# Second heads written to partitions 0 to 63, and a planner that counts the pause where the first partition changes

## The chip, the cores and the metric

The kernel runs on one core of a Trainium2 chip. The time is the device time of one execution in microseconds. Below, PE is TensorE's matmuls and PEld its weight loads, DVE is VectorE, ACT is ScalarE, POOL is GpSimd, and SP is SyncE, which here only issues DMAs.

## The reference

Attention with a decaying bias over 8 batches, 8 heads, 576 positions and 64 numbers a head, then a channel mix of the 512 joined numbers of each position with a hidden layer of 1024:

```python
scores = scale * np.matmul(q, k.transpose(0, 1, 3, 2))
cum = np.cumsum(np.maximum(s, 0.0), axis=-1)
bias = -(cum[:, :, :, None] - cum[:, :, None, :])
scores = np.where(causal, -1000000000.0, scores + np.minimum(bias, 0.0))
attn = np.exp(scores - np.max(scores, axis=-1, keepdims=True))
attn = attn / (np.sum(attn, axis=-1, keepdims=True) + 1e-09)
x = np.matmul(attn, v)          # heads joined: B, S, H * D
...
xk = mu_k * x + (1.0 - mu_k) * x_prev
xr = mu_r * x + (1.0 - mu_r) * x_prev
k = np.maximum(xk @ w_k, 0.0)
out = 1.0 / (1.0 + np.exp(-(xr @ w_r))) * (k * k @ w_v)
```

x_prev is x moved by one position.

## The kernel before

**Visits.** Attention goes over visits: one batch and one pair of heads. The first batch is done in two parts for each pair (eight visits in plain float32), the other seven batches in one visit for each pair, 28 in all, where each float32 operand is split into a rounded part and a rest (ph and pl for the weights of attention, the four column blocks of V for the values). A visit takes its two heads j = 0 and 1 one after the other. For each: PE multiplies queries and keys into a bank `s` (L743 plain, L754 split); DVE adds the mask, takes the row's extreme and frees the bank (L771, tile nm); ACT takes the exponential (L789); POOL divides by the sum (L803, L825); PE transposes the weights into a bank `t` (L847, L861); ACT and DVE split the transposed weights into ph and pl (L887 and L891 for whole blocks; L912, L916, L935, L943 and L955 for half blocks, of which one half lies on partitions 64 to 127 of the bank); PE multiplies them with the values into a bank `po` or the rest of a `t` bank (L995 plain, L1011 split); and ACT (L1041; L1034 plain) and DVE (L1045) add the two halves of that bank into xT.

**xT.** It is a tile of 128 partitions: head 0 of the pair on partitions 0 to 63, head 1 on 64 to 127. In the split visits ACT copies one half of the bank, the rows of the rest of V, to the head's partitions and DVE adds the other half. For head 0 ACT reads from partition 64 and writes at 0 and DVE stays at 0; for head 1 ACT reads from 0 and writes at 64, and DVE reads and writes at 64. The plain product of L995 multiplies the values of both heads and copies the rows of the one it wants. When both heads are done, one DMA (L1347) writes xT to x_d in DRAM.

**Mixing.** The 18 chunks of 256 positions read x_d back into the one tile x (L1240). For each pair of 128 channels ACT scales x by mu into the bank `xp` (L1087) and DVE adds the neighbour's share (L1096); a bank takes two such ACT steps and two DVE steps (more where a chunk lies across two batches), then ACT rounds the bank into xh (L1115) and DVE takes the rest xl (L1119). There is one `xp` bank. PE multiplies into the two `m` banks (L1148 hidden layer, L1190 gate, L1215 output); ACT and DVE square the hidden layer in four steps, r (L1160), m (L1170), kh (L1175) and kl (L1177), after which the bank is free; DVE joins gate and output (L1226), and a DMA writes the result (L1232). DVE, ACT and PE wait for each other through semaphores, also where two of them touch different parts of one bank.

**The planner.** No instruction is issued where the code names it. Each becomes a task with an engine, a length and what it reads and writes, and `Plan.run` simulates all engines with a table of costs, forward and backward in turn for eight passes, and issues all tasks in the order of the shortest pass. In each step the engine that is free first takes its most urgent ready task. SELF is the time from the end of a task to a dependent one on the same engine, AFTER and BEFORE the parts of it across engines. The order thus found is the order of every engine, the DMAs' SP included. A part of a buffer is named by a pair, as `(xm, (y, o))`; two tasks depend on each other where one writes a part that the other names.

## Time and profile before

| what | value |
|---|---|
| median of 3 runs | 890.72 us (886.85 to 893.18) |
| the profiled execution | 892.16 us |
| its span, first to last instruction | 890.4 us |
| mean granted clock of TensorE | 0.992 of full speed |
| busy: PE, PEld | 854.3 us (96%), 741.1 us (83%) |
| busy: DVE, ACT, POOL | 668.8 us (75%), 677.5 us (76%), 423.3 us (48%) |

Busy time is the union of an engine's instructions. Matmuls are pipelined, so a busy PE may still be slower than it could be. In a timeline, a line gives the start from the span's beginning, the length, and in square brackets the idle time before it with what ended it; the end of an instruction is its start plus its length, and where the next one starts before that, the two overlap. A wait names the engine and line that waited, the one that released it, the total in us, how often, and the longest.

### The profile page before, as it was taken

Reading aid. Unit: us, or ns where it says so; the run is one execution under the profiler, and the core shown is the slowest. Engines: PE = TensorE matmul, PEld = TensorE weight load, DVE = VectorE, ACT = ScalarE, POOL = GpSimd, SP = SyncE. Lnnn points to the kernel's source line nnn. Section 1 sums busy time; section 2 is a strip of 40 time slices with the busy share of each in tenths; the row PEclk is TensorE's granted clock in tenths of the full one; section 3 lists DMA queues with packets and bytes.
Section 4 is the critical chain, followed back from the end, with each engine's and each line's share of the span. In section 5 each row is a group of like instructions: output and inputs, shape, how many; then the busy total and the mean of one; then the engine's idle time right before and its main releaser. Section 6 shows DMA issues by size and latency. Waiting matters only on the chain.

```text
span 890.4 us, 16963 instructions
## 1 busy us (share of the span) xinstructions
PE 854.3 (96%) x5353; PEld 741.1 (83%) x5353; DVE 668.8 (75%) x2190; ACT 677.5 (76%) x1810; POOL 423.3 (48%) x654
## 2 busy tenths in 40 slices
PE   8899999999999999999999999989999999998998
PEld 6678788779798888979897989888888879987886
DVE  6989898789777887778877786868787768445431
ACT  5988999989878887888878787878787868346331
POOL 7655877865546455545455545443544532000000
PEclk8989999999999999999999999999999999999999
DMA  7887355453544525333334443242435110111100
GB/s 195 272 237 219 94 162 142 108 155 102 128 130 108 143 77 154 88 109 100 113 93 110 116 124 109 76 132 61 135 82 144 43 62 14 42 33 35 48 26 24
DMA packets 52762, 96.70 MB, mean 109 GB/s; under 512 B 7502, under 2 KB 20820, under 8 KB 52672
## 3 DMA queue, kind: packets, MB, share of 16 engines
q1 hardware_dynamic: 52672, 95.62, 38.5%
q8 instruction: 42, 0.69, 0.3%
q14 instruction: 48, 0.39, 0.2%
HBM read 67.85 MB, written 19.48 MB: 98 GB/s over the span
## 4 chain that ended last, share of the span: by engine, by line
PE 54%; DVE 18%; ACT 18%; issue 5%; DMA 2%; POOL 2%; SPq 1%; ACTq 0%; DVEq 0%; POOLq 0%
PE m L1148 17%; PE m L1215 11%; PE m L1190 7%; PE s L754 5%; PE po L1011 5%; ACT W L789 4%; DVE W L771 4%; PE t L847 4%; DVE xp L1096 4%; ACT xp L1087 3%; DVE pl L891 3%; ACT ph L887 3%; DMA x<-x_d 2%; DVE xT L1045 2%; PE po L995 1%
## 5 line engine op out<-in xcount | busy, mean ns | idle before, releaser
L1148 PE MATMUL m<-xh,w_k 128*128 128x256 f32 x1152 | 231.1, 286 | 2.5 <-DVE kl L1177 2.4
L789 ACT ACTIVATE W<-W,nm 128x448 f32<-128x448 f32 (+4 forms) x320 | 179.1, 561 | 27.8 <-DVE nm L771 24.4
L1215 PE MATMUL m<-w_v,kh 128*128 128x512 f32 x576 | 198.9, 403 | 0.4 <-DVE r L556 0.4
L1148 PEld LDWEIGHTS m<-xh,w_k 128*128 128x128 f32 x1152 | 185.8, 188 | 5.2 <-DVE kl L1177 2.7
L803 POOL TENSOR_SCALAR W<-W,rinv 128x192 f32<-128x192 f32 (+4 forms) x320 | 164.4, 532 | 32.7 <-DVE rinv L830 30.2
L1148 PE MATMUL m<-xl,w_k 128*128 128x256 f32 x576 | 163.2, 283 | 0.2 <-DVE xl L1119 0.2
L771 DVE CUSTOM_DVE_ANT_0 W<-s,causal 64x64 f32<-64x64 f32 (+4 forms) x320 | 128.3, 409 | 24.2 <-PE s L754 15.4
L1215 PEld LDWEIGHTS m<-w_v,kh 128*128 128x128 f32 x576 | 106.6, 188 | 18.0 <-DVE r L556 0.8
L891 DVE TENSOR_TENSOR pl<-t,ph 128x512 fp32r<-128x512 f32 x224 | 104.3, 485 | 19.7 <-ACT ph L887 18.1
L1215 PE MATMUL m<-w_v,kl 128*128 128x512 f32 x288 | 115.0, 399 | 0.0
L1096 DVE SCALAR_TENSOR_TENSOR xp<-x,mu,xp 128x256 f32<-128x256 f32 (+3 forms) x192 | 80.7, 420 | 44.6 <-ACT xp L1087 41.7
L847 PE MATMUL t<-ident,W 128*128 128x128 f32 x640 | 111.7, 276 | 2.1 <-POOL W L803 0.8
L754 PE MATMUL s<-KH,G 128*64 128x64 f32 x336 | 101.5, 310 | 11.3 <-DVE nm L771 11.2
L1087 ACT ACTIVATE xp<-x,mu 128x256 f32<-128x256 f32 (+3 forms) x192 | 81.5, 424 | 37.8 <-DVE xl L1119 13.4
L1148 PEld LDWEIGHTS m<-xl,w_k 128*128 128x128 f32 x576 | 108.5, 188 | 1.6 <-DVE xl L1119 0.6
L722 POOL TENSOR_TENSOR G<-raw,G 64x1152 fp32r<-64x1152 f32 x28 | 75.0, 2678 | 58.6 <-issue 42.3
L1190 PE MATMUL m<-w_r,xh 128*128 128x512 f32 x288 | 101.9, 405 | 0.1
L754 PE MATMUL s<-KL,G 128*64 128x64 f32 x336 | 97.9, 294 | 0.0
L887 ACT CAST ph<-t 128x512 fp32r<-128x512 f32 x224 | 89.1, 426 | 11.0 <-PE t L847 5.6
L847 PEld LDWEIGHTS t<-ident,W 128*128 128x128 f32 x640 | 80.1, 142 | 16.0 <-issue 2.9
L1011 PE MATMUL po<-ph,V 128*128 128x448 f32 x280 | 85.1, 319 | 4.5 <-ACT ph L887 4.2
L825 POOL TENSOR_SCALAR rinv<-sums 128x5 f32<-128x5 f32 (+2 forms) x72 | 17.3, 240 | 141.7 <-ACT W L789 138.8
(112 smaller groups left out, 1742.7 us busy)
## 6 DMA issues: line engine op xcount, KB each, us to landing
raw<-in_q SPq DMA_DIRECT2D x56, 288.0 KB
raw<-in_k SPq DMA_DIRECT2D x56, 288.0 KB
out<-g SPq DMA_DIRECT2D x36, 256.0 KB
vn<-in_v SPq DMA_DIRECT2D x28, 320.0 KB
x_d<-xT SPq DMA_DIRECT2D x28, 288.5 KB
G<-G SPq DMA_DIRECT2D x28, 288.0 KB
x<-x_d SPq DMA_DIRECT2D x12, 514.0 KB
w_k<-in_moe_w_k SPq DMA_DIRECT2D x8, 512.0 KB
```

The costliest lines, as they stand in the source:

```text
L754: lambda x=x, g=g, K=K: nc.tensor.matmul(ps.get()[:m, :w], g.get()[:, h % 2, q0 : q0 + m], K.get()[:, h % 2, k0 : k0 + w], start=x == 0, s ...
L771: lambda a=a, e=e, at=at, i=i: nc.vector.tensor_tensor_reduce(out=W.ap[:m, at : at + e - a], in0=ps.get()[:m, a - k0 : e - k0], in1=causal ...
L789: lambda: nc.scalar.activation(W.ap[:m, :n], W.ap[:m, :n], AF.Exp, bias=nm.get()[:m, 3 * t + mi : 3 * t + mi + 1], scale=-1.0, accum_out=s ...
L803: lambda: nc.gpsimd.tensor_scalar(out=to, in0=W.ap[:m, :n], scalar1=rinv.get()[:m, t : t + 1], scalar2=1.0, op0=ALU.mult, op1=ALU.mult,),
L847: lambda: nc.tensor.transpose(ps.get()[0:m, place : place + P], pt[t].ap[:, lead(t) + k0 : lead(t) + k0 + m], ident.ap),
L887: act(lambda: nc.scalar.copy(strips(ph), src()), [ps], [(ph, k) for k in ks], n * m)
L891: lambda: nc.vector.tensor_tensor(out=strips(pl), in0=src(), in1=f32(strips(ph)), op=ALU.subtract),
L1011: lambda: nc.tensor.matmul(po.get()[: P if both else 64, at + q0 - base : at + q0 - base + m], V.get()[:, kb, 2 * j : 2 * j + (2 if both e ...
L1096: lambda n=n, o=o, i=i, to=to: nc.vector.scalar_tensor_tensor(out=to(), in0=x.get()[:, c, o + i : o + i + n], scalar=mu1.ap[:, which, c : ...
L1148: lambda u=u, f=f, c=c, n=n, w=w, x=x: nc.tensor.matmul(ps.get()[:, u * CT : (u + 1) * CT], weight["k", c, f // 4].get()[:, w, f % 4 * P : ...
L1190: lambda c=c, n=n, x=x, w=w: nc.tensor.matmul(ps.get(), x.get()[:, c, ts], weight["r", c, 0].get()[:, w], start=c == 0 and n == 0, stop=c ...
L1215: lambda f=f, n=n, x=x, w=w: nc.tensor.matmul(ps.get(), x.get()[:, f, ts], weight["v", f, 0].get()[:, w], start=f == 0 and n == 0, stop=f ...
```

## The change

xT becomes a tile of 64 partitions with a second dimension for the head, so that both heads of a pair lie on partitions 0 to 63. In the split visits ACT reads from partition 64 and DVE adds from partition 0 for either head. The plain product takes one head's 64 columns of V. The DMA to x_d reads 64 partitions with two rows each.

The planner gets a short text for every ACT and most DVE tasks that says which memories it reads and writes and from which partition ("P64>S": from partition 64 of PSUM to partition 0 of SBUF). It keeps, for ACT and DVE, the first partition of the last read and write in each memory. A task for which one of them differs counts as held and is simulated 122 ns (ACT) or 108 ns (DVE) later; and of the up to four most urgent ready tasks the engine takes the one with the least due time, where a held one counts 200 ns later. SELF of DVE goes from 127 to 185 ns. In the mixing, the ACT steps of one bank now depend on each other through the part "a", the DVE steps through "d".

```diff
@@ -56,18 +57,20 @@
-    SELF = {"PE": 0.0, "ACT": 150.0, "DVE": 127.0, "POOL": 62.0, "SP": 0.0}
+    SELF = {"PE": 0.0, "ACT": 150.0, "DVE": 185.0, "POOL": 62.0, "SP": 0.0}
...
+    HELD, LOOK, AVOID = {"ACT": 122.0, "DVE": 108.0}, 4, 200.0
...
@@ -95,6 +98,27 @@
+
+    def side(self, i, ports):
+
+        if ports is None:
+            return
+        ins, out = (
+            [(x[0], int(x[1:] or 0)) for x in re.findall("[PS][0-9]*", part)] for part in ports.split(">")
+        )
+        self.ports[i] = ins, out
+
+    def held(self, i, state):
+
+        ins, out = self.ports.get(i, ((), ()))
+        return any(state["R" + m] != p for m, p in ins) or any(state["W" + m] != p for m, p in out)
+
+    def moved(self, i, state):
+        ins, out = self.ports.get(i, ((), ()))
+        for m, p in reversed(ins):
+            state["R" + m] = p
+        for m, p in out:
+            state["W" + m] = p
 
     def add(self, engine, ns, emit, reads=(), writes=(), land=0.0):
         i = len(self.tasks)
...
@@ -139,6 +163,7 @@
+        states = {e: dict.fromkeys(("RP", "RS", "WP", "WS"), 0) for e in self.HELD}
...
@@ -191,6 +216,19 @@
                     if x is not best:
                         heapq.heappush(ready[e], x)
                 i = best[1]
+            if e in self.HELD:
+                if ready[e]:
+                    some = [(due[i], i)]
+                    while ready[e] and len(some) < self.LOOK:
+                        some.append(heapq.heappop(ready[e]))
+                    best = min(some, key=lambda x: x[0] + self.AVOID * self.held(x[1], states[e]))
+                    for x in some:
+                        if x is not best:
+                            heapq.heappush(ready[e], x)
+                    i = best[1]
+                if self.held(i, states[e]):
+                    s += self.HELD[e]
+                self.moved(i, states[e])
             _, ns, _, _, _, land = self.tasks[i]
             if e == "PE":
 
...
@@ -339,11 +377,15 @@
-    def act(emit, reads, writes, n, extra=51, table=0):
-        return plan.add("ACT", n * 0.8333 + extra, emit, reads, writes, land=table)
-
-    def dve(emit, reads, writes, n, rate=0.96):
-        return plan.add("DVE", n / rate + 68, emit, reads, writes)
+    def act(emit, reads, writes, n, extra=51, table=0, ports=None):
+        i = plan.add("ACT", n * 0.8333 + extra, emit, reads, writes, land=table)
+        plan.side(i, ports)
+        return i
+
+    def dve(emit, reads, writes, n, rate=0.96, ports=None):
+        i = plan.add("DVE", n / rate + 68, emit, reads, writes)
+        plan.side(i, ports)
...
@@ -958,7 +1001,7 @@
                             in1=f32(ph.get()[0:64, c]),
                             op=ALU.subtract,
                         ),
-                        [ps, (ph, ("h", k1))], [(ph, "l")], 64,
+                        [ps, (ph, ("h", k1))], [(ph, "l")], 64, ports=f"P{64 * r}S>S64",
                     )
 
         def turned(*what):
...
@@ -986,21 +1029,19 @@
         else:
             turned((0, 2))
             turned([(3, 4)], (2,), (3,))
-        lo, ot = 64 * j, 64 * (1 - j)
-
         def values(po, base, at, kb, q0, m, x, first, last):
             parts = [("h", kb), "l" if kb == NQ - 1 else kb]
             if plain:
                 i = pe(
                     lambda: nc.tensor.matmul(
-                        po.get()[:, at + q0 - base : at + q0 - base + m],
-                        V.get()[:, kb],
+                        po.get()[0:64, at + q0 - base : at + q0 - base + m],
+                        V.get()[:, kb, j],
                         x.get()[:, col(kb, q0) : col(kb, q0) + m],
                         start=first,
                         stop=last,
                     ),
                     [V] + [(x, i) for i in parts[: 2 if kb < NQ - 1 else 1]],
-                    [po], m, P, 4 / 2.4,
+                    [po], m, 64, 4 / 2.4,
                 )
                 if plan.busy_from is None:
                     plan.busy_from = i
...
@@ -1031,24 +1072,22 @@
             n = q1 - q0
             if plain:
                 act(
-                    lambda: nc.scalar.copy(
-                        xT.get()[lo : lo + 64, 1 + q0 : 1 + q1], po.get()[lo : lo + 64, at : at + n]
-                    ),
-                    [po], [(xT, (j, q0))], n,
+                    lambda: nc.scalar.copy(xT.get()[:, j, 1 + q0 : 1 + q1], po.get()[0:64, at : at + n]),
+                    [po], [(xT, (j, q0))], n, ports="P>S",
                 )
                 return
             act(
-                lambda: nc.scalar.copy(xT.get()[lo : lo + 64, 1 + q0 : 1 + q1], po.get()[ot : ot + 64, at : at + n]),
-                [po], [(xT, (j, q0))], n,
+                lambda: nc.scalar.copy(xT.get()[:, j, 1 + q0 : 1 + q1], po.get()[64:P, at : at + n]),
+                [po], [(xT, (j, q0))], n, ports="P64>S",
             )
             dve(
                 lambda: nc.vector.tensor_tensor(
-                    out=xT.get()[lo : lo + 64, 1 + q0 : 1 + q1],
-                    in0=po.get()[lo : lo + 64, at : at + n],
-                    in1=xT.get()[lo : lo + 64, 1 + q0 : 1 + q1],
+                    out=xT.get()[:, j, 1 + q0 : 1 + q1],
+                    in0=po.get()[0:64, at : at + n],
+                    in1=xT.get()[:, j, 1 + q0 : 1 + q1],
                     op=ALU.add,
                 ),
-                [po], [(xT, (j, q0))], n,
+                [po], [(xT, (j, q0))], n, ports="PS>S",
             )
 
         for q0, q1 in sums_of(tiles):
...
@@ -1090,7 +1129,7 @@
                         AF.Copy,
                         scale=mu.ap[:, which, c : c + 1],
                     ),
-                    [(x, i), (mu, which)], [(xm, (y, o))], n, 160,
+                    [(x, i), (mu, which)], [(xm, (y, o)), (xm, "a")], n, 160, ports="S>P",
                 )
                 dve(
                     lambda n=n, o=o, i=i, to=to: nc.vector.scalar_tensor_tensor(
@@ -1101,7 +1140,7 @@
                         op0=ALU.mult,
                         op1=ALU.add,
                     ),
-                    [(x, i), mu1], [(xm, (y, o))], n,
+                    [(x, i), mu1], [(xm, (y, o)), (xm, "d")], n, ports="SP>P",
                 )
 
         def splits(c, xm, hi, lo):
...
@@ -1344,7 +1383,9 @@
 
             c = slice(1 + q0 if q0 else 0, 1 + q1)
             dma(
-                lambda: nc.sync.dma_start(x_d[b].ap[:, hp, c], xT.get()[:, c]),
+                lambda: nc.sync.dma_start(
+                    x_d[b].ap[:, hp, c].rearrange("(h d) t -> d h t", h=2), xT.get()[:, :, c]
+                ),
                 [(xT, 2)] + [(xT, (i, x)) for i in range(2) for x, _ in sums_of(tiles)],
                 [(x_d[b], (hp, y)) for y in range(2) if tiles is ALL or y == (q0 > 0)],
                 819,
@@ -1359,8 +1400,8 @@
         if 0 < n < len(visits) - 1:
             load(n + 1)
         plan.due = due
-        xT = sbuf([P, S + 1], "xT", 2)
-        pool(lambda xT=xT: nc.gpsimd.memset(xT.get()[:, 0:1], 0.0), [], [(xT, 2)], 1, 36)
+        xT = sbuf([64, 2, S + 1], "xT", 2)
+        pool(lambda xT=xT: nc.gpsimd.memset(xT.get()[:, :, 0:1], 0.0), [], [(xT, 2)], 2, 36)
         for j in range(2):
             plan.due = due + j * step
             pt = scores(b, 2 * hp + j, tiles, *QKs[n])
```

The order of every engine comes out anew. Lines of the changed kernel have other numbers: L985 is L943, L998 is L955, L933 is L891, L813 is L771, L1126 is L1087, L1154 is L1115, L1199 is L1160, L1209 is L1170, L1214 is L1175.

The first place is on DVE, in a split visit of the first half of the program, where the halves of the transposed weights are taken: the L943 of 64x64 and L955 (L985 and L998) both read the upper half of the bank. In brackets stand the semaphores that an instruction waits for, named by engine or DMA queue. Before:

```order
L943 TENSOR_TENSOR pl<-t_296,ph_1232 64x64
L771 ISA W_72,nm_202<-s_169,causal,nm_202 128x64 [waits DVE_49]
L771 ISA nm_202 128x1
L891 TENSOR_TENSOR pl<-t_296,ph_1232 128x256
L955 TENSOR_TENSOR ph_1232<-t_296,ph_1232 64x64
L891 TENSOR_TENSOR pl<-t_237,ph_1232 128x384 [waits PE_49,Activation_49]
L891 TENSOR_TENSOR pl<-t_237,ph_1232 128x128
```

and now:

```order
L933 TENSOR_TENSOR pl<-t_287,ph_1242 128x256
L813 ISA W_72,nm_202<-s_169,causal,nm_202 128x64 [waits DVE_49]
L813 ISA nm_202 128x1
L985 TENSOR_TENSOR pl<-t_287,ph_1242 64x64
L998 TENSOR_TENSOR ph_1242<-t_287,ph_1242 64x64
L1209 SCALAR_TENSOR_TENSOR m_221<-m_221,r_832 128x512 [waits Activation_49]
L933 TENSOR_TENSOR pl<-t_240,ph_1242 128x384 [waits PE_49,Activation_49]
```

One reduction of a score with its read-out and a whole block stood between the two reads of partition 64; now these stand next to each other. Over the whole program L955 stands right behind L943 in 16 of 56 cases before, and L998 right behind L985 in 45 of 56 now.

The second place is on ACT in the last stretch of the program, when attention is over: the mixing of a chunk that lies across two batches (four steps into one bank, of 192 and 64 positions) and the first hidden bank m_176 of the chunk in front. Before:

```order
L1115 CAST xh_782<-xp_294 128x512 [waits DVE_49]
L1087 ACTIVATE xp_294<-x_611,mu 128x192 [waits DVE_49]
L1087 ACTIVATE xp_294<-x_611,mu 128x64 [waits Activation_49]
L1087 ACTIVATE xp_294<-x_611,mu 128x192 [waits DVE_49]
L1087 ACTIVATE xp_294<-x_611,mu 128x64 [waits DVE_49]
L1160 ACTIVATE r_789<-m_176 128x512 [waits PE_49]
L1115 CAST xh_782<-xp_294 128x512 [waits DVE_49]
L1175 CAST kh_213<-m_176 128x512 [waits DVE_49]
L1160 ACTIVATE r_789<-m_220 128x512 [waits PE_49,Activation_49]
```

and now:

```order
L1154 CAST xh_814<-xp_274 128x512 [waits DVE_49]
L1199 ACTIVATE r_832<-m_176 128x512 [waits PE_49]
L1126 ACTIVATE xp_274<-x_640,mu 128x192 [waits DVE_49]
L1126 ACTIVATE xp_274<-x_640,mu 128x64 [waits Activation_49]
L1126 ACTIVATE xp_274<-x_640,mu 128x192 [waits DVE_49]
L1214 CAST kh_212<-m_176 128x512
L1126 ACTIVATE xp_274<-x_640,mu 128x64 [waits DVE_49]
L1199 ACTIVATE r_832<-m_221 128x512 [waits PE_49]
L1154 CAST xh_814<-xp_274 128x512 [waits DVE_49]
```

r of the bank stood behind the four mixing steps and stands ahead of them now, and its cast kh stood behind the cast xh and now stands behind three of the four steps.

The third place follows on it directly: the mixing of the next chunk, whose first step waits for the load into x (DMAHW0). Before:

```order
L1175 CAST kh_213<-m_220 128x512 [waits DVE_49]
L1087 ACTIVATE xp_294<-x_611,mu 128x256 [waits DMAHW0_49]
L1087 ACTIVATE xp_294<-x_611,mu 128x256 [waits Activation_49]
L1160 ACTIVATE r_789<-m_176 128x512 [waits PE_49]
L1175 CAST kh_213<-m_176 128x512 [waits DVE_49]
L1160 ACTIVATE r_789<-m_220 128x512 [waits PE_49,Activation_49]
L1115 CAST xh_677<-xp_294 128x512
```

and now:

```order
L1214 CAST kh_212<-m_221 128x512 [waits DVE_49]
L1199 ACTIVATE r_832<-m_176 128x512 [waits PE_49,Activation_49]
L1126 ACTIVATE xp_274<-x_640,mu 128x256 [waits DMAHW0_49,DVE_49]
L1214 CAST kh_212<-m_176 128x512 [waits DVE_49]
L1126 ACTIVATE xp_274<-x_640,mu 128x256 [waits DVE_49]
L1199 ACTIVATE r_832<-m_221 128x512 [waits PE_49,Activation_49]
L1154 CAST xh_709<-xp_274 128x512 [waits DVE_49]
```

The two mixing steps stood next to each other, the second waiting for ACT itself; now r stands ahead of them and a cast between them, and the second waits for a step of DVE.

## Rows read from the trace of the kernel before

**Rows 1.** The page's part 1: busy us (share of the span) xinstructions of each engine.

```profile
PE 854.3 (96%) x5353; PEld 741.1 (83%) x5353; DVE 668.8 (75%) x2190; ACT 677.5 (76%) x1810; POOL 423.3 (48%) x654
```

**Rows 2.** The page's part 4: the chain that ended last, shares of the span.

```profile
PE 54%; DVE 18%; ACT 18%; issue 5%; DMA 2%; POOL 2%; SPq 1%; ACTq 0%; DVEq 0%; POOLq 0%
PE m L1148 17%; PE m L1215 11%; PE m L1190 7%; PE s L754 5%; PE po L1011 5%; ACT W L789 4%; DVE W L771 4%; PE t L847 4%; DVE xp L1096 4%; ACT xp L1087 3%; DVE pl L891 3%; ACT ph L887 3%; DMA x<-x_d 2%; DVE xT L1045 2%; PE po L995 1%
```

**Rows 3.** Busy time by stretch: PE, PEld, DVE, ACT, POOL, clock, DMA share, GB/s.

```profile
300.00:500.00 200.00, 194.63 (x1285) 173.80 (x1284) 159.49 (x547) 165.04 (x441) 109.94 (x158) 1.00 0.42 115
...
783.00:891.00 108.00, 100.94 (x571) 86.84 (x569) 42.74 (x75) 38.10 (x74) 0.00 (x0) 1.00 0.10 34
```

**Rows 4.** The waits of PE: engine line, whom for, us, times, longest.

```profile
PE s L754 <- DVE nm L771: 11.2, 21, 1.1
PE m L1148 <- DVE kl L1177: 2.4, 1, 2.4
```

**Rows 5.** Timeline of DVE from 409.5: start us, us, what.

```profile
409.50 0.17 DVE L830 RECIPROCAL rinv<-rinv 128x5 f32<-128x5 f32 x1
409.70 0.23 DVE L943 TENSOR_TENSOR pl<-t,ph 64x64 fp32r<-64x64 f32 x1
409.94 0.42 DVE L891 TENSOR_TENSOR pl<-t,ph 128x256 fp32r<-128x256 f32 x1
410.38 0.23 DVE L955 TENSOR_TENSOR ph<-t,ph 64x64 fp32r<-64x64 f32 x1
410.64 0.70 DVE L1170 SCALAR_TENSOR_TENSOR m<-m,r 128x512 f32<-128x512 f32 x1
```

**Rows 6.** Timeline of DVE at three other places.

```profile
389.98 0.63 DVE L1045 TENSOR_TENSOR xT<-po,xT 64x448 f32<-64x448 f32 x1 [0.19 <-ACT xT L1041]
390.64 0.42 DVE L1096 SCALAR_TENSOR_TENSOR xp<-x,mu,xp 128x192 f32<-128x192 f32 x1
...
402.11 1.02 DVE L1096 SCALAR_TENSOR_TENSOR xp<-x,mu,xp 128x256 f32<-128x256 f32 x2 [0.42 <-ACT xp L1087]
...
404.93 0.62 DVE L1045 TENSOR_TENSOR xT<-po,xT 64x448 f32<-64x448 f32 x1 [0.41 <-ACT xT L1041]
405.47 0.44 DVE L771 CUSTOM_DVE_ANT_0 W<-s,causal 128x288 f32<-128x288 f32 x1
```

**Rows 7.** Timeline of ACT from 404.4.

```profile
404.38 0.51 ACT L1041 COPY xT<-po 64x448 f32<-64x448 f32 x1
404.92 0.60 ACT L1160 ACTIVATE r<-m 128x512 f32<-128x512 f32 x1
405.42 0.66 ACT L789 ACTIVATE W<-W,nm 128x448 f32<-128x448 f32 x1
```

**Rows 8.** The waits of DVE and ACT inside the mixing.

```profile
DVE xp L1096 <- ACT xp L1087: 41.7, 60, 4.9
...
ACT xp L1087 <- DVE xp L1096: 9.9, 18, 2.2
```

**Rows 9.** Groups by line and shape: busy us, mean ns, idle before.

```profile
L1096 DVE SCALAR_TENSOR_TENSOR xp<-x,mu,xp 128x256 f32<-128x256 f32 x96 | 46.7, 486 | 20.0 <-ACT xp L1087 18.5
...
L995 PEld LDWEIGHTS po<-ph,V 128*128 128x128 f32 x128 | 24.6, 208 | 8.3 <-ACT ph L912 3.0 <-ACT ph L887 0.7 <-issue 0.6
```

**Rows 10.** Timeline of ACT, DVE and PE in the last stretch.

```profile
802.48 0.43 ACT L1087 ACTIVATE xp<-x,mu 128x192 f32<-128x192 f32 x1 [0.49 <-DVE xp L1096]
803.51 0.58 ACT L1160 ACTIVATE r<-m 128x512 f32<-128x512 f32 x1
...
805.62 0.68 DVE L1177 TENSOR_TENSOR kl<-m,kh 128x512 fp32r<-128x512 f32 x1
...
806.35 0.38 PE L1148 MATMUL m<-xh,w_k 128*128 128x256 f32 x1 [2.37 <-DVE kl L1177]
```

**Rows 11.** Busy time of two short stretches, columns as in rows 3.

```profile
630.10:631.60 1.50, 1.50 (x11) 1.36 (x10) 0.82 (x3) 1.48 (x6) 1.50 (x1) 1.00 0.65 203
...
783.60:784.60 1.00, 1.00 (x6) 0.81 (x5) 0.00 (x0) 0.13 (x1) 0.00 (x0) 1.00 0.75 295
```

More of the change, by code (lines that the diff above doesn't have):

```diff
@@ L70, in __init__ @@
         self.columns, self.idle, self.busy_from = {}, None, None
+        self.ports = {}
     def buffer(self, pool, shape, dtype, tag, bufs):
@@ L796, in exponents @@
                 ),
-                [(nm, (t, mi))], [(W, i) for i in range(3)] + [(sums, t)], n, 280, 1,
+                [(nm, (t, mi))], [(W, i) for i in range(3)] + [(sums, t)], n, 280, 1, "S>S",
             )
@@ L886, in block @@
             ks = range(kb, kb + n)
-            act(lambda: nc.scalar.copy(strips(ph), src()), [ps], [(ph, k) for k in ks], n * m)
+            act(lambda: nc.scalar.copy(strips(ph), src()), [ps], [(ph, k) for k in ks], n * m, ports="P>S")
             if plain:
@@ L893, in block @@
                 ),
-                [ps] + [(ph, k) for k in ks], [(pl, k) for k in ks], n * m,
+                [ps] + [(ph, k) for k in ks], [(pl, k) for k in ks], n * m, ports="PS>S",
             )
@@ L935, in halves @@
                     lambda ks=ks, src=src: nc.scalar.copy(strips_of(ph, ks), src()),
-                    [ps], [(ph, x) for x in parts], n,
+                    [ps], [(ph, x) for x in parts], n, ports=f"P{64 * r}>S",
                 )
@@ L1115, in splits @@
                 lambda: nc.scalar.copy(hi.get()[:, cc], src()),
-                parts, [(hi, c), (hi, c + 1)], 2 * CT,
+                parts, [(hi, c), (hi, c + 1)], 2 * CT, ports="P>S",
             )
@@ L1121, in splits @@
                 ),
-                parts + [(hi, c), (hi, c + 1)], [(lo, c), (lo, c + 1)], 2 * CT,
+                parts + [(hi, c), (hi, c + 1)], [(lo, c), (lo, c + 1)], 2 * CT, ports="PS>S",
             )
@@ L1228, in output @@
                 ),
-                [ps], [g], DM,
+                [ps], [g], DM, ports="SP>S",
             )
```

19 lines of the change are left out of this document (11 added, 8 removed).

## The prediction

> **What bounds the kernel now.** I read the page's busy shares first, then the chain, then stretches of time, then the waits of the busiest engine. PE is busy 96% of the span, DVE and ACT about three quarters each [rows 1], so at first sight PE is the bound and nothing else counts. The chain corrects this: it runs over PE for 54% of the span only, over DVE for 18% and over ACT for 18% [rows 2]. 18% of 890.4 us is 160 us; DVE is busy 668.8 us and ACT 677.5 us [rows 1], so about 0.24 of what either of them does lies on the path, and 0.76 lies beside other work. The stretches say where. From 300 to 500 us, with attention and mixing side by side, DVE is busy 159 and ACT 165 of 200 us and PE idles 5.4 us; from 783 us on, when attention is over, PE idles 7.1 of 108 us, what follows its last matmul included, while DVE and ACT have less than half a load [rows 3]. Among PE's own waits the largest is that of the scores (L754) for the reduction L771, which frees their bank: 11.2 us in 21 waits. One wait of 2.4 us stands alone [rows 4]; it belongs to the last stretch.
>
> **The pause.** The timeline shows the thing that the planner now counts. L943 on 64x64 and L955 read the upper half of a PSUM bank, from partition 64. Of five DVE instructions in a row, the first starts at 409.50 and ends at 409.67; L943 starts at 409.70, 0.03 us later. L891, back at partition 0, starts at 409.94, 0.01 us after L943's end; L955 0.02 us after the end of that, and L1170 0.03 us after L955 [rows 5]. Where the first partition stays, an instruction starts before the end of the one in front: L771 at 405.47, while L1045 ends at 405.55 [rows 6]. The pause on DVE is thus 0.08 + 0.02 to 0.03 us; I take 0.105. On ACT L1160 starts at 404.92, 0.03 us after L1041, which read partition 64, and the next starts 0.10 us before L1160's end [rows 7]; I take 0.13.
>
> **Part by part.** (1) *Pauses.* The L1045 of a second head reads and writes from partition 64; the one at 389.98 is followed by a start 0.03 us after its end, that of a first head at 404.93 is not [rows 6]. There are 56 of the second kind, two pauses at the most each, and all go. The planner further sets L955 right behind L943: in 16 of 56 cases before, in 45 now, as the first place in the order shows. Going along the whole order of each engine by the first partition of every operand, I count 321 pauses on DVE before and 211 now, 334 on ACT before and 274 now. On ACT the halves that were written at 64 are gone, but all copies of L1041's kind now read from 64, so less is won there. 110 x 0.105 = 11.6 us on DVE, 60 x 0.13 = 7.8 us on ACT, 19.4 us together. How much of it counts? Between nothing, if all lies beside PE's work, and all of it. 36 of DVE's stand directly ahead of L771 (57 before, 21 now), the instruction PE waits for most; those 36 x 0.105 = 3.8 us I count in full, and the other 15.6 us at the chain's 0.24, 3.7 us. Together -7.5 us.
>
> (2) *Mixing.* The new dependences through the parts "a" and "d" hold the scaled copies of one bank in order, and the planner answers with more alternation: an ACT step behind a DVE step of the same bank 44 times before and 68 now, a DVE step behind an ACT step 116 and 140. In the trace these changes of engine cost idle time: 41.7 us on DVE, which is 0.36 us for each of the 116, and 9.9 us on ACT, 0.225 us for each of the 44 [rows 8]. 24 x (0.36 + 0.225) = 14.0 us of idle time more. Against it, 24 pairs fewer stand back to back on one engine. Such a pair waits for itself: two L1096 take 1.02 us [rows 6] where one takes 0.486 [rows 9], so 0.05 us lie between them instead of an overlap of 0.08; 0.13 us a pair, on both engines 24 x 2 x 0.13 = 6.2 us. Net +7.8 us of engine time, +1.9 us at 0.24. The ends are nothing and the full 24 x (0.70 + 0.55) = 30 us, if each of them idles as long as those 60 and 18 that did.
>
> (3) *The last stretch.* PE's single wait of 2.37 us ends at 806.35, when kl of L1177 has ended (806.30) [rows 10]. Its chain began with L1160's r at 803.51, which stood behind four mixing activations; now it stands ahead of them and the cast to kh behind three, as the second place in the order shows. The third of the four ended at 802.91 [rows 10]; with 0.58 us for r put in front it ends at 803.49, the cast of 0.58 us at 804.07, kl of 0.68 us at 804.75. That is 1.5 us earlier, and as PE has nothing else there, -1.5 us; between 0 and -2.4. The third place shows what follows: the next r, too, is now ahead of the activations that wait for the load into x, and its cast stands behind one of them instead of two, so that nothing of the gain is lost there by the order.
>
> (4) *Weights of the plain products.* 128 loads of 208 ns take half the columns now [rows 9]. At half the time that would be 13 us of weight loading. I count it at nothing, because PEld runs beside PE's matmuls; without this cover, up to 13 us in the first stretch.
>
> (5) *The output's transfer.* It now leaves from 64 partitions. For 288.5 KB from 128 partitions one window of 1.0 us holds the whole transfer at 295 GB/s; a load of 288 KB into 64 partitions needs 1.5 us at 203 GB/s [rows 11]. So about 0.5 us more for each of 28, 14 us in all, on a queue that is not on the path: the chain has 2% for DMA [rows 2], and the bank it frees is cleared by POOL, busy 48% [rows 1]. I count 0. The Trainium skill ("SBUF — State Buffer", section on the DMA port swizzle) speaks against this layout: partitions 0 to 63 reach no more ports than 0 to 31, and it states 196 GB/s at 1 MiB against 328 from 128 partitions. The trace agrees in direction, 203 against 295; by the page's figures a transfer would take 1.7 times as long, and the sum would be the same 0 as long as it is covered.
>
> The added clearing of two elements for one, and the one more warming matmul at the start, are nothing. All other matmuls are the same in number and size.
>
> **Sum.** -7.5 + 1.9 - 1.5 = -7.1 us on the profiled execution's 892.16 us: 885.1. That execution is 1.4 us above the median of the runs, so against the median 890.72 it is 883.6 us, 0.8% faster. A measurement here tells no more than about 1%, that is 881.8 below and 899.6 above. How far a planner with truer costs places its work better or worse beyond these counts, no row tells; both engines' orders are new from end to end. I give it 5 us to each side, near half of PE's largest wait [rows 4]: 877 to 889.
>
> **Rivals.** *The pauses count in full.* Then 19.4 + 2.4 = 21.8 us go and the mixing costs nothing: 869 us; with four fifths of it, 873. For it speaks that three engines are above 75% in the middle [rows 3], and that where DVE is late PE waits. Against it: 0.76 of DVE's work is off the chain. *Alternation wins (slower).* The mixing chain goes back and forth between ACT and DVE through one bank, and both engines are held in order behind each wait. At the full price of 30 us, and with half of it on the path, +15, the other terms being -6.2 (all 19.4 us at 0.24, and the last stretch): 899.5, up to 903. It decides when more than 0.2 of the 30 us are on the path, since 0.2 x 30 is those 6 us. L1096 and L1087 hold 7% of the chain already [rows 2]; against it, the planner alternates where it has other work to set between. *Nothing moves.* PE's columns are the same, and DVE and ACT merely idle more: 890, give or take 2. *The transfer counts.* A slow write holds up loads behind it on the one queue: 28 x 0.5 = 14 us on top of the -7.1, 897.6 us. The DMA's 2% of the chain speaks against it. It is what the page on SBUF, named above, would lead one to expect.
>
> **Chances.** Forecast 0.56, of which 0.23 lie below 881.8. Pauses in full 0.15. Nothing moves 0.11. Alternation 0.13, of which 0.10 above 899.6. The transfer 0.05, 0.02 of it above. Faster by over 1%: 0.23 + 0.15 = 0.38; slower: 0.10 + 0.02 = 0.12; within: 0.50. For 8 in 10 the range takes the forecast's own 877 to 889, the unmoved case, four fifths of the first rival at 873 and the beginning of the slower one: 872 to 898.
>
> **What the changed profile would show.** If (1) is right, DVE's and ACT's busy times hardly change, but the starts after a second head's sum lie 0.08 us before its end, and the scores' wait for L771's successor falls below 11.2 us. If (2) is right, the wait of ACT's mixing step for DVE's rises from 18 times toward 28 and more, and DVE's for ACT's from 60 upward. If (3) is right, PE has no wait over 1.5 us after 783 us. I would be wrong if PE's idle time (36 us) stays although pauses are fewer, which would say that the path does not run through DVE where they stood, or if new waits of the kind of the 2.37 us appear elsewhere; a planner that avoids pauses puts other work off, by up to its 200 ns each time.

## The result and the profile after

| | before | after |
|---|---|---|
| median | 890.14 us (886.85 to 893.18, 4 executions) | 868.73 us (868.02 to 874.13, 4 executions) |
| profiled execution, span | 892.16 us, 890.4 us | 874.13 us, 872.4 us |
| mean granted clock in it | 0.992 | 0.982 |

The ratio is 0.9762 [0.9728, 0.9796]: 2.4% faster, 21 us, where 7 were forecast. A comparison leaves out executions more than 1.5% above the fastest of the same kernel, which ran at a lower mean clock.

The page of the kernel after: busy times, the clock in 40 slices, the chain. Lines have moved by about 40: the scores' L754 is L796, the reduction L771 is L813, the mixing steps L1087 and L1096 are L1126 and L1135.

```profile
PE 856.1 (98%) x5354; PEld 738.4 (85%) x5354; DVE 658.9 (76%) x2190; ACT 669.1 (77%) x1810; POOL 424.0 (49%) x654
...
PEclk8679999999999999999999999999999999999999
...
PE 86%; DVE 4%; ACT 4%; DMA 2%; issue 2%; POOL 1%; SPq 0%; POOLq 0%; DVEq 0%; ACTq 0%
```

Against [rows 1, 2]: busy times are much as they were, and the chain has left DVE and ACT. It ran over them for 36% of the span and runs over them for 8%. The gain is in what PE waits for. Stretches of the kernel after (PE, PEld, DVE, ACT, POOL, clock, DMA share, GB/s):

```profile
0.00:120.00 120.00, 113.01 (x528) 73.52 (x529) 94.31 (x281) 89.45 (x262) 72.64 (x129) 0.87 0.65 189
...
300.00:500.00 200.00, 200.00 (x1353) 182.35 (x1352) 162.41 (x570) 169.35 (x460) 111.70 (x161) 1.00 0.47 119
...
120.00:700.00 580.00, 576.04 (x3823) 518.83 (x3822) 476.06 (x1699) 501.37 (x1369) 338.45 (x499) 1.00 0.46 117
...
120.00:765.60 645.60, 641.48 (x4255) 577.22 (x4254) 520.82 (x1832) 540.57 (x1474) 351.33 (x526) 1.00 0.43 109
```

From 300 to 500 us PE idled 5.4 us [rows 3]; now it doesn't idle at all and issues 1353 matmuls instead of 1285. Attention ends at 765.6 us instead of 782.1. The same stretches of the kernel before:

```profile
0.00:120.00 120.00, 111.95 (x600) 88.38 (x601) 103.00 (x320) 102.38 (x291) 84.53 (x147) 0.94 0.70 204
...
120.00:700.00 580.00, 560.16 (x3672) 494.83 (x3670) 464.44 (x1619) 482.49 (x1300) 317.35 (x470) 1.00 0.42 113
...
120.00:782.10 662.10, 640.52 (x4183) 565.13 (x4181) 522.16 (x1795) 536.43 (x1445) 338.74 (x508) 1.00 0.38 104
```

Between 120 us and the end of attention PE idled 662.10 - 640.52 = 21.6 us and now 645.60 - 641.48 = 4.1 us. That is 17.5 us, and the spans differ by 18.0; the last stretch gives 1.5 us (108.3 us behind attention before, 106.8 now). But idle time does not tell all. In the first 120 us, with the clock lower (0.87 instead of 0.94), PE issues 528 matmuls instead of 600, so 72 more are left to the stretch behind: 4255 instead of 4183. At the 0.153 us that one took there before (640.52 / 4183) they are 11 us of work, by estimate; the stretch does them as well and is still 16.5 us shorter. So it gained some 28 us, a part of it inside PE's busy time (0.151 us a matmul now), and the start gave some 11 back. What PE waits for after:

```profile
PE s L785 <- DVE nm L813: 3.4, 4, 1.7
PE s L796 <- DVE nm L813: 2.3, 4, 1.0
...
PE po L1052 <- ACT ph L929: 1.3, 1, 1.3
PE m L1187 <- DVE kl L1216: 0.9, 1, 0.9
```

The 21 waits of 11.2 us of the split scores [rows 4] are 4 of 2.3 us; those of the plain scores rose from 1.7 to 3.4 us. The start is worse: the first slices of the clock read 8679, and two stretches of it, 30.8 us together, ran at half the full clock, 1.2 of 2.4 GHz:

```profile
0.00:14.70 14.70, 11.90 (x62) 8.02 (x63) 8.68 (x29) 6.32 (x17) 12.20 (x35) 1.00 0.70 195
14.70:35.20 20.50, 20.29 (x62) 11.05 (x60) 13.82 (x51) 11.88 (x46) 7.96 (x20) 0.50 0.53 167
35.20:55.60 20.40, 18.00 (x85) 10.02 (x84) 19.28 (x58) 18.84 (x67) 13.18 (x27) 1.00 0.82 237
55.60:65.90 10.30, 10.00 (x25) 5.07 (x26) 6.35 (x19) 5.00 (x15) 4.61 (x7) 0.50 0.96 274
```

### The profile page after: what moved, and what is told of

It is laid out like the page before. It is cut to its first block, busy times and chain, and to the rows that moved or that the text cites. A ratio compares the mean times of both kernels' runs of the same rounds, so it can differ in the third digit from the quotient of the medians.

```text
span 872.4 us, 16950 instructions
## 1 busy us (share of the span) xinstructions
PE 856.1 (98%) x5354; PEld 738.4 (85%) x5354; DVE 658.9 (76%) x2190; ACT 669.1 (77%) x1810; POOL 424.0 (49%) x654
## 4 chain that ended last, share of the span: by engine, by line
PE 86%; DVE 4%; ACT 4%; DMA 2%; issue 2%; POOL 1%; SPq 0%; POOLq 0%; DVEq 0%; ACTq 0%
PE m L1187 22%; PE m L1254 20%; PE m L1229 11%; PE s L796 9%; PE po L1052 8%; PE t L889 7%; PE po L1036 3%; PE s L785 3%; PE t L903 2%; DMA x<-x_d 1%; PE t L1052 1%; DVE xp L1135 1%; DVE W L813 1%; PE po L401 1%; ACT xp L1126 1%
## 5 line engine op out<-in xcount | busy, mean ns | idle before, releaser
L813 DVE CUSTOM_DVE_ANT_0 W<-s,causal 128x448 f32<-128x448 f32 (+4 forms) x320 | 128.3, 409 | 45.4 <-PE s L796 26.7
L933 DVE TENSOR_TENSOR pl<-t,ph 128x512 fp32r<-128x512 f32 x224 | 103.5, 481 | 20.7 <-ACT ph L929 17.4
L1135 DVE SCALAR_TENSOR_TENSOR xp<-x,mu,xp 128x256 f32<-128x256 f32 (+3 forms) x192 | 80.3, 418 | 36.9 <-ACT xp L1126 33.9
L1126 ACT ACTIVATE xp<-x,mu 128x256 f32<-128x256 f32 (+3 forms) x192 | 81.4, 424 | 31.5 <-DMA x<-x_d 12.1
L796 PE MATMUL s<-KH,G 128*64 128x64 f32 x336 | 98.2, 304 | 2.4 <-DVE nm L813 2.3
L796 PE MATMUL s<-KL,G 128*64 128x64 f32 x336 | 97.7, 296 | 0.0
## 6 DMA issues: line engine op xcount, KB each, us to landing
x_d<-xT SPq DMA_DIRECT2D x28, 288.5 KB
```

The source lines that it names most:

```text
L796: lambda x=x, g=g, K=K: nc.tensor.matmul(ps.get()[:m, :w], g.get()[:, h % 2, q0 : q0 + m], K.get()[:, h % 2, k0 : k0 + w], start=x == 0, s ...
L813: lambda a=a, e=e, at=at, i=i: nc.vector.tensor_tensor_reduce(out=W.ap[:m, at : at + e - a], in0=ps.get()[:m, a - k0 : e - k0], in1=causal ...
L933: lambda: nc.vector.tensor_tensor(out=strips(pl), in0=src(), in1=f32(strips(ph)), op=ALU.subtract),
L1126: lambda n=n, o=o, i=i, to=to: nc.scalar.activation(to(), x.get()[:, c, o + i + 1 : o + i + 1 + n], AF.Copy, scale=mu.ap[:, which, c : c + 1],
```

## Experiments

The theory after the result: the **order** gained it, since a planner that counts what DVE's and ACT's steps take sets them so that PE doesn't wait; the pauses that the new layout removes are a small part. The rival is the prediction's own: the **pauses** that go are time won. A second question came later: must the planner count the pauses where they stand (C), or does any length added to the plan do (M), or is it **scatter**, any other order being as likely to be this good?

All results together. The ratio is to the kernel before, measured beside it. "Idle" is PE's idle time from 120 to 700 us in the profiled execution. The last column has the executions at the highest mean clocks of each kernel; "none" stands where none reached 0.996. Each planned kernel is a single order.

| kernel | ratio [95%] | idle, us | us (clock) |
|---|---|---|---|
| before | | 19.8 | 887.1 to 888.1 (1.000) |
| after | 0.9762 [0.9728, 0.9796] | 4.0 | none, 868.0 to 869.0 (0.988 to 0.990) |
| layout_old_order | 0.9984 [0.9963, 1.0004] | 16.2 | 884.8 (1.000) |
| new_order_old_layout | 0.9758 [0.9730, 0.9785] | 5.8 | 867.6 (0.997) |
| planner_old_layout | 0.9785 [0.9753, 0.9816] | 6.7 | none, 868.6 (0.993) |
| none_of_planner | 0.9937 [0.9920, 0.9953] | 15.4 | 885.2, 885.6 (0.998) |
| no_avoid | 0.9783 [0.9765, 0.9801] | 7.2 | 871.8 (0.998) |
| no_held_no_avoid | 0.9866 [0.9827, 0.9905] | 11.9 | 876.7, 877.7 (1.000) |
| self127 | 0.9786 [0.9751, 0.9821] | 3.7 | 868.2, 871.0 (0.998) |
| no_ad | 0.9884 [0.9850, 0.9918] | 10.3 | 877.7 (0.998) |
| before_counting | 0.9846 [0.9808, 0.9885] | 8.1 | 874.4, 875.8 (0.996) |
| before_ad | 1.0011 [0.9977, 1.0046] | 16.7 | 889.5 to 891.1 (0.998) |
| uniform_pause | 0.9845 [0.9803, 0.9888] | 8.4 | 875.4 (0.997) |
| no_ad_longer | 0.9835 [0.9785, 0.9885] | 8.3 | 874.6 (0.996) |
| scatter_after | none (two executions) | 7.3 | none, 874.0, 874.5 (0.988) |
| scatter_no_held | 0.9888 [0.9844, 0.9932] | 13.0 | 875.8, 878.3 (1.000) |
| held_double | 0.9963 [0.9944, 0.9982] | 7.3 | none, 886.0 to 888.4 (0.960 to 0.963) |
| warm_more | 0.9770 [0.9696, 0.9843] | 2.9 | 862.3 (1.000) |
| self127_warm | 0.9768 [0.9750, 0.9785] | 4.6 | 871.0 to 872.7 (0.997 to 0.998) |
| true_step_warm | 0.9758 [0.9715, 0.9800] | 2.7 | 862.2 (1.000) |

### Layout and order, each alone

layout_old_order is the kernel before, its order kept row for row, with the outputs of both heads on partitions 0 to 63.

```diff
-        xT = sbuf([P, S + 1], "xT", 2)
+        xT = sbuf([64, 2, S + 1], "xT", 2)
...
-                    out=xT.get()[lo : lo + 64, 1 + q0 : 1 + q1],
-                    in0=po.get()[lo : lo + 64, at : at + n],
+                    out=xT.get()[:, j, 1 + q0 : 1 + q1],
+                    in0=po.get()[0:64, at : at + n],
```

> Every engine keeps the order of the kernel before, row for row; only the layout of the change is taken (both heads on partitions 0 to 63, 64 columns of V in the plain product, the transfer from 64 partitions). Counted along the orders, pauses fall from 321 to 231 on DVE and from 334 to 298 on ACT. Theory P (the pauses themselves were on the path, in full): 90 x 0.105 + 36 x 0.13 = 14 us less, about 876 us, two thirds of the whole gain. Theory O (the new order is what counts): these pauses at the chain's share of 0.24 give 3 us, about 887 us. Theory T (the transfer from 64 partitions costs): slower than before.

new_order_old_layout is the reverse: the order of the kernel after, row for row, with the layout of before, so that the pauses are back. planner_old_layout lets the whole new planner plan the old layout with its true partitions (`f"P{lo}S{lo}>S{lo}"` for the second heads' sums).

> Every engine keeps the order of the changed kernel, row for row, but xT is laid out as before, so that the pauses of second heads come back: 292 on DVE and 317 on ACT, against 211 and 274 in the changed kernel. Theory P: 81 x 0.105 + 43 x 0.13 = 14 us of the gain are lost, about 883 us. Theory O: nearly all of the gain stays, 869 to 873 us.

> The whole planner of the change (pauses counted and avoided, 185 ns for DVE, parts a and d), with the old layout and its true first partitions; the planner makes its own order, with 309 pauses on DVE and 326 on ACT. Theory P: 12 and 8 pauses fewer than before are 2 us, about 888 us. Theory O: most of the gain, 870 to 876 us, since the planner knows of every pause that is left.

The new layout took 1.4 us (889.81 against 891.17 us), and its interval holds no change. By the order it has 90 pauses fewer on DVE and 36 on ACT (231 and 298 are left): 90 x 0.105 + 36 x 0.13 = 14.1 us of engine time. Little of it reaches the end: PE's idle time falls by 3.6 us, from 19.8 to 16.2. The two kernels were not at one clock; between executions of equal mean clock (0.990, 0.992 and 0.994) the layout is 2 to 3.5 us faster, by the means of the few there are. Its chain is much like that of before [rows 2], and its scores' wait is 7.6 us where it was 11.2 [rows 4]:

```profile
PE 58%; ACT 18%; DVE 15%; issue 4%; DMA 3%; POOL 1%; SPq 0%; ACTq 0%; DVEq 0%; POOLq 0%
```

```profile
PE s L754 <- DVE nm L771: 7.6, 15, 1.0
```

The new order with the old layout has the whole gain, and planner_old_layout most of it (873.32 us with 309 and 326 pauses by its order). That the pauses of new_order_old_layout are back is seen at one step, first in its DVE timeline, then in that of the kernel after:

```profile
382.87 0.63 DVE L1086 TENSOR_TENSOR xT<-po,xT 64x448 f32<-64x448 f32 x1
383.53 0.42 DVE L813 CUSTOM_DVE_ANT_0 W<-s,causal 128x256 f32<-128x256 f32 x1
```

```profile
389.36 0.60 DVE L1084 TENSOR_TENSOR xT<-po,xT 64x448 f32<-64x448 f32 x1
389.89 0.41 DVE L813 CUSTOM_DVE_ANT_0 W<-s,causal 128x256 f32<-128x256 f32 x1
```

L813 starts 0.03 us after the sum's end there (382.87 + 0.63 = 383.50) and 0.07 us before it here: the pause that went saved its 0.10 us of DVE, and little of that reached PE. The stretch of new_order_old_layout from 120 to 700 us, with the second heads' pauses back (292 on DVE and 317 on ACT by the order; 211 and 274 in the kernel after), is nearly that of the kernel after:

```profile
120.00:700.00 580.00, 574.25 (x3790) 513.85 (x3789) 477.47 (x1680) 497.67 (x1354) 332.20 (x488) 1.00 0.43 115
```

The rival *pauses* at its full price falls with these two runs; a price of about 2 us does not.

### Which part of the planner

Each takes one part from the kernel after; none_of_planner takes all four. What stays in it is the new layout with the old costs.

```diff
# no_avoid, no_held_no_avoid
-    HELD, LOOK, AVOID = {"ACT": 122.0, "DVE": 108.0}, 4, 200.0
+    HELD, LOOK, AVOID = {"ACT": 122.0, "DVE": 108.0}, 4, 0.0
+    HELD, LOOK, AVOID = {"ACT": 0.0, "DVE": 0.0}, 4, 0.0
# self127
-    SELF = {"PE": 0.0, "ACT": 150.0, "DVE": 185.0, "POOL": 62.0, "SP": 0.0}
+    SELF = {"PE": 0.0, "ACT": 150.0, "DVE": 127.0, "POOL": 62.0, "SP": 0.0}
# no_ad (the same for "d")
-                [(xm, (y, o)), (xm, "a")], n, 160, ports="S>P"
+                [(xm, (y, o))], n, 160, ports="S>P"
```

> The changed kernel with the old planner: no pause is counted or avoided, 127 ns for DVE, no parts a and d; the layout is new and the order differs from that of before only through the cost of the plain product and of a clearing. 229 pauses on DVE, 294 on ACT. Theory P: as the layout in the old order, about 876 us. Theory O: within 5 us of before, 885 to 890 us.

> The changed kernel, whose planner counts a pause (122 and 108 ns) but no longer avoids it (0 in place of 200 ns): 230 pauses on DVE and 300 on ACT, as many as with none of the planner's changes. Theory C (the order is better because the pauses are counted): the gain stays, 868 to 874 us. Theory A (avoiding them, which groups the accesses to the upper half, does it): 880 to 886 us. Theory S (neither; the costs of waiting for the own engine, 185 ns and the parts a and d, do it): the gain stays.

> The changed kernel, whose planner neither counts nor avoids pauses; 185 ns and the parts a and d stay. 229 pauses on DVE and 297 on ACT. Theory C: the gain is lost for the most part, 880 to 886 us. Theory A: the same. Theory S: the gain stays, 868 to 874 us.

> The changed kernel with 127 ns again for a dependent task on DVE; all else stays. 208 pauses on DVE, 277 on ACT. Theories C and A: the gain stays, 868 to 874 us. Theory S: some 5 to 10 us of it are lost, 875 to 880 us.

> The changed kernel without the parts a and d; all else stays. In the mixing an ACT step follows a DVE step 41 times in place of 68, nearly as in the kernel before (44). Theories C and A: the gain stays, 868 to 874 us, or grows a little if alternation costs. Theory S: 5 to 10 us are lost.

Without the four parts 0.6% is left of 2.4%. Without the counting of the pauses (no_held_no_avoid) or without the dependences "a" and "d" (no_ad) about half of the gain goes. Neither theory C nor theory S had both: no_held_no_avoid lies mostly between their ranges, and no_ad is where S had it and C did not. Without the passing over of held tasks (no_avoid, 0.9783) and without the longer SELF (self127, 0.9786) 0.2% is lost each, within the intervals, so theory A falls. The stretch without the counting shows where it goes: 3736 matmuls from 120 to 700 us instead of 3823.

```profile
120.00:700.00 580.00, 568.12 (x3736) 505.70 (x3735) 467.01 (x1652) 488.83 (x1330) 327.97 (x479) 1.00 0.45 115
```

Then each of the two alone, on the kernel before with its old layout: before_counting has only the counting (the old layout's true partitions, AVOID 0; the clearing of xT is planned as one of two elements), before_ad only the two dependences.

```diff
# before_counting, in Plan.run
+            if e in self.HELD:
+                if self.held(i, states[e]):
+                    s += self.HELD[e]
+                self.moved(i, states[e])
# before_ad
-                [(xm, (y, o))], n, 160,
+                [(xm, (y, o)), (xm, "a")], n, 160,
```

> The kernel before, whose planner counts pauses (122 and 108 ns, with the true first partitions of the old layout), and nothing else of the change: no avoiding, no parts a and d, 127 ns, old layout. 326 pauses on DVE and 325 on ACT are left, as many as before. Theory C: a good part of the gain, 876 to 883 us, with PE's idle time between 120 us and the end of attention falling from 21.6 to about 11 us. Theory P (fewer pauses): nothing, 890 us.

> The kernel before with the parts a and d, and nothing else of the change. An ACT step of the mixing follows a DVE step 68 times in place of 44, as in the changed kernel. Theory of the prediction's second term (alternation costs): 2 us slower than before, about 892 us. Theory D (the parts tell the planner a wait that the chip really has): 880 to 886 us.

Counting alone, with as many pauses left as before (326 on DVE, 325 on ACT), gives 875.86 against 891.89 us by the medians and 0.9846 by the ratio: 14 to 16 us of the 21. At a clock of 1.000 the counting and avoiding are worth as much: no_held_no_avoid takes 876.7 and 877.7 us there, and the order of the kernel after 862.3 (warm_more, one execution). The two dependences alone give nothing, against theory D; behind the counting they take PE's idle time from 10.3 us (no_ad) to 4.0. But no_ad, which counts the pauses too, is no faster than before_counting, so the parts do not add up, and this share of the dependences rests on one order. Pages of before_counting: the chain, and PE's waits for the scores' bank.

```profile
PE 73%; ACT 9%; DVE 7%; DMA 5%; issue 2%; POOL 2%; SPq 1%; ACTq 0%; POOLq 0%; DVEq 0%
```

```profile
PE s L796 <- DVE nm L813: 3.8, 9, 1.5
```

### Where the pauses stand, or any length, or scatter

uniform_pause counts no pause and makes every step a little longer, by about the mean of what the counting adds; no_ad_longer leaves "a" and "d" out and makes each mixing step 65 ns longer in the plan; held_double counts the pauses twice.

```diff
# uniform_pause (HELD and AVOID 0), in Plan.run
+            if e in self.HELD:
+                s += {"ACT": 24.0, "DVE": 15.0}[e]
# no_ad_longer
-                [(xm, (y, o)), (xm, "a")], n, 160, ports="S>P"
+                [(xm, (y, o))], n, 225, ports="S>P"
# held_double
+    HELD, LOOK, AVOID = {"ACT": 244.0, "DVE": 216.0}, 4, 200.0
# scatter_after, scatter_no_held (the latter with HELD and AVOID 0)
-    AFTER = {"PE": 235.0, "ACT": 150.0, "DVE": 160.0, "POOL": 60.0, "SP": 1000.0}
+    AFTER = {"PE": 235.0, "ACT": 150.0, "DVE": 160.0, "POOL": 66.0, "SP": 1000.0}
```

> The changed kernel, whose planner neither counts nor avoids pauses at their places, but adds to every ACT task 24 ns and to every DVE task 15 ns, so that the same total (297 x 122 and 229 x 108 ns) is spread evenly. Theory C (the planner must know where a pause falls): as without counting, 877 to 883 us. Theory M (the planner was too hopeful about the two engines and any added time helps it): 868 to 874 us.

> The changed kernel without the parts a and d, but every mixing step of ACT and DVE is planned 65 ns longer, 130 ns a pair, the time that a pair waits for itself. Theory D (what the parts bring is that they say which steps follow each other): as without the parts, 877 to 884 us. Theory M: 868 to 874 us.

> The changed kernel, whose planner counts each pause with twice its length (244 and 216 ns). Theory C (the true length at the true place is what helps): not faster than the changed kernel, 868 to 878 us, with more idle time on PE. Theory M (any added time helps): PE's idle time falls further, below 4 us between 120 us and the end of attention.

> The changed kernel with one unrelated cost of the planner moved a little (66 in place of 60 ns behind a POOL task), which makes a new order of the same quality. Theories C and M: 867 to 874 us, like the changed kernel. Theory L (the differences between the orders are luck): anywhere between 868 and 886 us.

> The kernel that neither counts nor avoids pauses (185 ns and the parts a and d stay), with the same unrelated cost moved. Theories C and M: 876 to 884 us, like that kernel without the move. Theory L: anywhere between 868 and 890 us.

A length without a place seems to give some of it: PE's idle time is 8.4 us in uniform_pause, between 11.9 without and 7.2 with the counting (no_avoid); its ratio, 0.9845, is that of before_counting, and the ratios' intervals overlap. no_ad_longer lies between no_ad and the kernel after in the same way. So C and M are not settled: part of the gain may be mere length. Scatter is not the whole cause. Another order without the counting (scatter_no_held) takes 875.8 and 878.3 us at clock 1.000 where the first takes 876.7 and 877.7, and the six kernels whose order knows neither a counted pause nor an added length idle 11.9 to 19.8 us, the thirteen whose order counts pauses 2.7 to 10.3. Yet another order with the counting (scatter_after) is 874.0 us at clock 0.988 where the kernel after is 868.0, and idles 7.3 us against 4.0: so some 6 us of time, and 3 us of idle time, hang on chance. held_double misses in time because its first stretch ran at the lower clock. From 120 to 700 us it idles 7.3 us, as much as no_avoid and more than the 4.0 of the kernel after: theory M, which had it below 4, missed, but scatter_after idles as much without a wrong length.

```profile
13.00:77.80 64.80, 63.85 (x162) 31.72 (x163) 40.63 (x136) 36.80 (x126) 30.08 (x60) 0.50 0.63 183
...
120.00:700.00 580.00, 572.74 (x3802) 516.33 (x3801) 477.32 (x1692) 500.88 (x1362) 340.34 (x499) 1.00 0.46 118
```

### The clock at the start

warm_more is the kernel after with more warming matmuls at the start, 73 instead of 50; the orders of the other engines are the same. self127_warm has this and self127 (93 of them), true_step_warm both and a DVE mixing step that is 61 ns longer in the plan.

```diff
-    TARGET, GAP = 5000.0, 250.0
+    TARGET, GAP = 8000.0, 100.0
```

> The changed kernel with its order, pauses and mixing as they are; only the warming matmuls at the start rise from 50 to 73. Theory W (the first 65 us cost part of the gain, because PE stands at the lower clock there for 30 us of the profiled execution): the lower clock covers less of the first 65 us and the time falls by some 3 to 8 us, to 861 to 866 us. Rival: the lower clock comes later, behind the last warming matmul (22 us), and the time stays.

> The changed kernel with 127 ns for a dependent task on DVE, as before the change, and the greater number of warming matmuls. If the 185 ns bring nothing and the lower clock of the first 65 us is what is left to win: 862 to 868 us. If the warming matmuls only move the lower clock: 868 to 874 us, like the changed kernel.

> The same, but the planner gives each mixing step of DVE 61 ns more, since L1096 on 128x256 occupies DVE for 486 - 90 = 396 ns where the planner counts 335. Theory C (the nearer the costs are to the chip's, the better the order): PE's idle time between 120 us and the end of attention at 4 us or below, 860 to 868 us. Rival: no difference from the kernel without it.

None beats the kernel after beyond the intervals. self127_warm kept a clock of 0.997 to 0.998 in all its executions and still takes 871.0 to 872.7 us. warm_more's single executions are 862.3 us at clock 1.000, 872.8 at 0.986, 873.7 at 0.982 and 876.8 at 0.980, so that theory W's 861 to 866 us came out once in four; its profiled one had the lower clock from 29.0 to 59.7 us all the same. So the warming matmuls don't keep the clock up reliably, but the run shows what it costs: 10.5 us between two executions of one order. Where the clock stayed up (true_step_warm), PE issues 305 matmuls in its first 65 us, 78 of them warming ones, and 227 with 50 warming ones in the kernel after, so 50 more that do work:

```profile
0.00:65.00 65.00, 60.07 (x305) 36.51 (x306) 56.60 (x181) 49.91 (x162) 44.41 (x96) 1.00 0.83 240
```

```profile
0.00:65.00 65.00, 59.29 (x227) 33.68 (x228) 47.22 (x151) 41.16 (x139) 37.46 (x87) 0.77 0.73 212
```

## Why the prediction was wrong

The side was right, the size was not. **The step that failed** is the one behind the sum: "How far a planner with truer costs places its work better or worse beyond these counts, no row tells ... I give it 5 us to each side." That placement, put at nothing with 5 us to each side, is most of the gain. Counting alone, with as many pauses left, gave 14 to 16 us; the new order with the second heads' pauses back gave 20. And a row did tell how much there was to win: PE's idle time, 36 us in the span, 21.6 of it between 120 us and the end of attention. The prediction used it only as a sign, and took as its bound near half of PE's largest group of waits, the 11.2 us of [rows 4]. All waits of PE in that stretch could fall, and its idle time there fell by 17.5 us.

**(1) Pauses**, -7.5 us. The 0.10 us each was right on DVE, as the two timelines of L813 show. The layout takes 126 of the 170 counted pauses, and they are worth 1.4 us with an interval from 3.3 us to none, or 2 to 3.5 us at equal clock. The chain's share of 0.24 would give 3.4 of their 14.1 us and is not excluded. What the 3.8 us counted in full were worth, for the 36 pauses ahead of L771, was not tried by itself; leaving out the avoiding cost 0.2% (no_avoid). *The pauses count in full* named 869 us, which is the measured time, for a cause that the two runs of layout and order exclude: that it came out is luck.

**(2) Mixing**, +1.9 us: not borne out. By the order DVE and ACT alternate more often, as counted, yet they wait less for each other than in [rows 8], and leaving out the dependences that make them alternate costs time (no_ad, 0.9884 instead of 0.9762):

```profile
DVE xp L1135 <- ACT xp L1126: 33.9, 46, 6.2
...
ACT xp L1126 <- DVE xp L1135: 7.7, 21, 0.5
```

DVE's waits were to rise above 60 and ACT's from 18 toward 28; they are 46 and 21, and the longest of ACT's fell from 2.2 to 0.5 us. The price of an alternation was taken from the waits of the old order and did not hold in the new one. In the old planner (before_ad) the dependences change nothing, 1.0011, and its interval holds the 1.9 us as well. *Alternation wins* is excluded by the time.

**(3) The last stretch**, -1.5 us: right. The wait of 2.37 us [rows 10] is 0.88 us:

```profile
788.26 0.38 PE L1187 MATMUL m<-xh,w_k 128*128 128x256 f32 x1 [0.88 <-DVE kl L1216]
```

**(4) Plain weights**, 0: not tried by itself; it is part of the layout's 1.4 us. The 128 loads of half the columns took 17.0 us in layout_old_order, not half of the 24.6 us of [rows 9]:

```profile
L995 PEld LDWEIGHTS po<-ph,V 128*64 128x64 f32 x128 | 17.0, 150 | 16.3 <-issue 4.1 <-ACT ph L912 3.0 <-ACT ph L887 1.7
```

**(5) The transfer**: right that it costs nothing measurable, and nearly right in size, 0.6 us more where 0.5 were forecast. The last one of the kernel after moves its 288.5 KB in 1.6 us, and POOL's wait for it rises from 8.2 to 24.9 us:

```profile
767.60:769.20 1.60, 1.60 (x9) 1.33 (x8) 0.00 (x0) 0.60 (x1) 0.00 (x0) 1.00 0.84 183
```

```profile
POOL xT L1404 <- DMA x_d<-xT: 24.9, 14, 9.0
```

POOL is busy 49%, and its longer wait does not show in the time: layout_old_order has the same wait of 24.6 us and is no slower than the kernel before. The rule of the Trainium skill that the prediction weighed ("SBUF — State Buffer", section on the DMA port swizzle) is borne out in the rate, 183 GB/s in this window, and not in the time of the kernel.

**What stays open**: which of the planner's choices between before and after keep PE fed, whether the place of the counted pauses matters beyond their length, and how much of the dependences' share is scatter of the orders. That the plan is better because its DVE and ACT run as late as the chip's is argued from before_counting and uniform_pause, not shown step by step.

## What to carry to other kernels

In a kernel whose order comes from a planner, price a change of the planner's costs by the idle time of the engine that should never idle (here 21.6 us), not only by the work that the costs describe: here counting the cost was worth 14 to 16 us and removing 14.1 us of it from the engines 1.4. Test the two apart, by the old work in the new order and the new work in the old order. And look at the first stretch's clock before a gain or a loss is put down to the order: at equal clock the new order is worth some 25 us (887.1 to 888.1 in four executions of the kernel before and 862.3 in one of warm_more, all at 1.000), and 21 are measured. That is more than the 21.6 us of idle time, so idle time is a guide and not a bound: part of the gain lay inside PE's busy time.

## What the runs showed of the hardware

TensorE's clock in the first 80 us differs between orders and between executions of one order, and it costs more than most edits here: the kernel before takes 887.1 to 888.1 us at a mean clock of 1.000 and 890.8 to 894.6 us at 0.992, about 0.6 us for each 0.001; true_step_warm takes 862.2 us at 1.000 and 873.5 at 0.984, about 0.7. By these two, held_double's 886.6 us at 0.961 would hide an order of some 859 to 863 us, an estimate beyond the clocks it comes from. In all its executions the clock was 0.960 to 0.963, while that of warm_more went from 0.980 to 1.000 between executions of one program; what decides that is open. In the profiled execution of the kernel after, the clock fell at 14.7 us after a stretch in which PE was busy 11.90 of 14.70 us, and again at 55.6 after one with 18.00 of 20.40 us.

A change of the first partition costs an engine 0.10 us on DVE and 0.13 on ACT here, as the timelines show, but 126 such pauses fewer in one order moved the time by 1.4 us of 891.
